# Attention and a gated FFN in one kernel: exponentials as the stationary operand, bursts of whole query groups, hardware-queue loads and turns by DMA transposes

## The chip, the cores and the metric

The kernel runs on one core of a Trainium2 chip. The metric is the time of one execution on the device in microseconds (us). All times are of one core, so no die can be compared with another: a run of such a program is called slow here only when it lies more than 1.5% above the fastest run of the same kernel.

Engines in the profile: PE is TensorE (matmul), PEld its weight loads, DVE VectorE, ACT ScalarE, POOL GpSimd, SP SyncE. SPq and the other names with q are an engine's instruction queue, which here issues DMAs. PSUM is the memory that TensorE writes to. The granted clock (PEclk) is the share of TensorE's full clock that the profile reports. QK stands for the matmuls of the scores, AV for those of exponentials and values; to turn is to transpose.

## The reference

```
k_all, v_all = concat(beacon_k, k), concat(beacon_v, v)   # 16 beacon rows ahead of 576
scores = q @ k_all.T / sqrt(64)        # 8 batches, 8 heads, 576 queries, 592 keys, depth 64
scores = where(causal, -1e9, scores)   # beacon keys are never masked
a = exp(scores - max); a /= sum(a) + 1e-9
x = (a @ v_all) as [4608 tokens, 512]
out = (relu(x @ w_gate) * (x @ w_val)) @ w_out            # 512 -> 1536 -> 512, fp32 in and out
```

## The kernel before

Two heads make a pair; there are 4 pairs a batch, 32 in all. Keys lie on the partitions of the score tile, so the exponentials p have keys on partitions and queries on columns. A pair is worked in four steps. The FFN is cut into 9 tiles of 512 tokens, each of 12 "up" pieces (8 matmuls of 512 columns) and 4 "down" pieces (12 matmuls); one piece is put between the steps of attention as filler. The exponentials are not shifted by their maximum; a check of all sums at the end leads to a general path where they are out of range.

The parts that the change and the argument touch:

```python
# values and a block of ones are stationary, the exponentials stream twice
for half in range(2):
    for a in range(2):
        w = pr.v[:kr, kt, ...] if half == 0 else ones[:kr, :]        # 64 columns
        nc.tensor.matmul(o[rows, half, ...], w, p[:kr, a, c:c + n], ...)
...
nc.vector.reciprocal(r[:, :cn], o[:, 1, :cn])                        # 128 x 256: sums, repeated 64 times
nc.vector.tensor_mul(xT[:, pr.p_idx, t0:t0 + cn], o[:, 0, :cn], r[:, :cn])
...
def part(dst, p0, p1, t, src):                  # loads cast fp32 -> bf16 on the way, issued by POOL
    nc.gpsimd.dma_start(dst[p0:p1, t, c0:c1]..., src.rearrange("h p d -> p h d"))
...
for s in range(len(work) + LAG):                # one step
    if i == 0 and pr.p_idx == 0:                # at a batch's first step: all loads of the next batch
        load_qkv(pr.b + 1, 0, H, tiles[pr.b + 1])
    qk(pr, i)
    softmax(pr, i)                              # exp on ACT, then causal masks on POOL
    ...                                         # q, k of the next pair turned on TensorE (steps 2, 3)
    if ffn: ffn.pop(0)()                        # one FFN piece
    if s >= LAG: av(*work[s - LAG])
```

## Time and profile before

| | before |
|---|---|
| time, median of 2 | 592.45 us |
| TensorE busy (per-engine table) | 447.3 of 589.1 us |
| first FFN matmul group (timeline) | 114.6 us |
| TensorE's waits on masks (table of waits) | 111.0 us in 10 waits |
| one pair of attention on TensorE (timeline) | about 3.9 us |

The page of the kernel before: the per-engine table's start, then three rows of the picture in 40 equal slices, where each digit is the busy share in tenths.

```profile
PE 447.3 (76%) x4113; PEld 227.8 (39%) x4113; DVE 259.4 (44%) x369; ACT 194.9 (33%) x273; POOL 218.1 (37%) x458
...
PE   2000037859995999599969986997799999979995
...
POOL 9998262471246125621652174217411112000000
...
DMA  4669990190059006900890099009901100100102
```

TensorE starts late (the zeros), and later dips at regular distance; POOL is at its fullest where TensorE is empty. The chain of waits, followed back from the last instruction, by engine:

```profile
PE 66%; POOL 23%; DMA 6%; DVE 2%; issue 1%; ACT 1%; ACTq 0%; POOLq 0%; DVEq 0%
```

The table of waits, TensorE's rows (total us, times, longest):

```profile
PE aux L283 <- POOL p L264: 111.0, 10, 68.8
PE aux L236 <- DMA q_sb<-in_q_dram: 9.9, 5, 8.4
```

One of the dips in the timeline (start, length, engine, line, operation, output and input, count; in brackets the idle time before it). POOL works through the loads of the next batch, and the mask of the running step comes last:

```profile
353.64 4.26 POOL L207 DMA_DIRECT2D v_sb<-in_v_dram  x5
357.80 1.02 POOL L264 TENSOR_SCALAR_AFFINE_SELECT p<-p 128x224 bf16<-128x224 bf16 x3
358.36 0.42 PE L283 MATMUL aux<-p,v_sb 128*64 128x256 bf16 x2 [7.10 <-POOL p L264]
```

So TensorE waits 7.10 us for a mask that stood behind POOL's own load issues. That the queue is first in, first out is what the Trainium skill says ("PSUM — Partial Sum Buffer", Engine vs sequencer instructions), and this trace agrees: the mask starts when the last load has been issued.

Three groups of instructions (busy us, mean ns of one, idle time before):

```profile
L290 DVE RECIPROCAL r<-aux 128x256 f32<-128x256 f32 (+1 forms) x96 | 129.8, 1352 | 160.8 <-PE aux L283 160.7
...
L283 PE MATMUL aux<-p,v_sb 128*64 128x64 bf16 (+5 forms) x832 | 72.9, 240 | 116.3 <-POOL p L264 111.0
...
L207 POOL DMA_DIRECT2D v_sb<-in_v_dram x55 | 44.3, 907 | 1.7 <-DMA k_sb<-in_k_dram 1.5
```

And one step on TensorE in the timeline: AV from 331.29 us, QK from 331.80, an FFN piece from 332.09.

```profile
331.29 0.30 PE L283 MATMUL aux<-p,v_sb 128*64 128x256 bf16 x2
...
331.80 0.36 PE L254 MATMUL s<-qT,kT 64*128 64x256 bf16 x6
332.09 2.76 PE L323 MATMUL f<-wo,hT 128*128 128x512 bf16 x12
```

### The profile page before, as it was taken

Reading aid. Unit: us, or ns where it says so; the run is one execution under the profiler, and the core shown is the slowest. Engines: PE = TensorE matmul, PEld = TensorE weight load, DVE = VectorE, ACT = ScalarE, POOL = GpSimd, SP = SyncE. Lnnn points to the kernel's source line nnn. Section 1 sums busy time; section 2 is a strip of 40 time slices with the busy share of each in tenths; the row PEclk is TensorE's granted clock in tenths of the full one; section 3 lists DMA queues with packets and bytes.
Section 4 is the critical chain, followed back from the end, with each engine's and each line's share of the span. In section 5 each row is a group of like instructions: output and inputs, shape, how many; then the busy total and the mean of one; then the engine's idle time right before and its main releaser. Section 6 shows DMA issues by size and latency. Waiting matters only on the chain.

```text
span 589.1 us, 10169 instructions
## 1 busy us (share of the span) xinstructions
PE 447.3 (76%) x4113; PEld 227.8 (39%) x4113; DVE 259.4 (44%) x369; ACT 194.9 (33%) x273; POOL 218.1 (37%) x458
## 2 busy tenths in 40 slices
PE   2000037859995999599969986997799999979995
PEld 1000025525542554355435543553355555424442
DVE  0000027536733673376437543754476576432130
ACT  2000014324432543254425442543244454322321
POOL 9998262471246125621652174217411112000000
PEclk9999999779997999799979996999699999979998
DMA  4669990190059006900890099009901100100102
GB/s 31 40 41 138 202 115 2 14 112 2 3 94 102 1 3 102 94 1 20 96 82 2 21 108 69 2 22 120 57 2 38 39 1 10 65 0 19 53 2 75
DMA packets 127029, 29.45 MB, mean 50 GB/s; under 512 B 116608, under 2 KB 122368, under 8 KB 126976
## 3 DMA queue, kind: packets, MB, share of 16 engines
q0 software_dynamic: 121408, 19.15, 44.4%
q1 hardware_dynamic: 5568, 9.59, 4.4%
q8 instruction: 34, 0.56, 0.4%
q14 instruction: 19, 0.16, 0.1%
HBM read 38.27 MB, written 9.44 MB: 81 GB/s over the span
## 4 chain that ended last, share of the span: by engine, by line
PE 66%; POOL 23%; DMA 6%; DVE 2%; issue 1%; ACT 1%; ACTq 0%; POOLq 0%; DVEq 0%
PE f L308 16%; PE f L314 15%; PE f L323 14%; PE aux L283 11%; POOL v_sb L207 8%; POOL k_sb L207 7%; PE s L254 6%; POOL q_sb L207 5%; DMA wo<-in_moe_w_out_dram 4%; PE aux L236 2%; DMA k_sb<-in_k_dram 2%; PE aux L244 2%; DVE r L290 1%; POOL p L264 1%; ACT p L261 1%
## 5 line engine op out<-in xcount | busy, mean ns | idle before, releaser
L290 DVE RECIPROCAL r<-aux 128x256 f32<-128x256 f32 (+1 forms) x96 | 129.8, 1352 | 160.8 <-PE aux L283 160.7
L261 ACT ACTIVATE p<-s 128x832 bf16<-128x832 f32 (+2 forms) x128 | 110.4, 863 | 245.3 <-PE s L254 245.3
L264 POOL TENSOR_SCALAR_AFFINE_SELECT p<-p 128x224 bf16<-128x224 bf16 (+3 forms) x224 | 67.7, 334 | 273.2 <-ACT p L261 273.2
L283 PE MATMUL aux<-p,v_sb 128*64 128x64 bf16 (+5 forms) x832 | 72.9, 240 | 116.3 <-POOL p L264 111.0
L308 PE MATMUL f<-xT,wg 128*128 128x512 bf16 x432 | 119.5, 400 | 5.0 <-DVE xT L292 4.3
L316 DVE TENSOR_TENSOR hT<-g,f 128x512 bf16<-128x512 f32 x108 | 74.0, 685 | 107.5 <-PE f L314 105.6
L314 PE MATMUL f<-xT,wv 128*128 128x512 bf16 x432 | 114.5, 389 | 0.9 <-DVE hT L316 0.9
L283 PEld LDWEIGHTS <-v_sb 128*64 128x64 bf16 (+1 forms) x832 | 45.6, 116 | 167.6 <-issue 160.1
L323 PE MATMUL f<-wo,hT 128*128 128x512 bf16 x432 | 98.4, 380 | 0.0
L311 ACT ACTIVATE g<-f 128x512 f32<-128x512 f32 x108 | 64.4, 596 | 70.1 <-PE f L308 68.7
L314 PEld LDWEIGHTS <-wv 128*128 128x128 bf16 x432 | 43.4, 100 | 64.4 <-issue 19.3
L283 PE MATMUL aux<-p,ones 128*64 128x64 bf16 (+5 forms) x832 | 64.9, 234 | 0.0
L323 PEld LDWEIGHTS <-hT 128*128 128x128 bf16 x432 | 40.1, 98 | 46.7 <-issue 1.5
L308 PEld LDWEIGHTS <-wg 128*128 128x128 bf16 x432 | 36.9, 100 | 41.6 <-issue 10.6
L254 PE MATMUL s<-qT,kT 64*128 64x64 bf16 (+3 forms) x832 | 49.2, 233 | 0.6 <-DVE kT L246 0.6
L207 POOL DMA_DIRECT2D q_sb<-in_q_dram x55 | 44.2, 890 | 8.0 <-DMA wo<-in_moe_w_out_dram 6.8
L207 POOL DMA_DIRECT2D k_sb<-in_k_dram x55 | 43.8, 858 | 5.7 <-DMA wg<-in_moe_w_gate_dram 3.5
L283 PEld LDWEIGHTS <-ones 128*64 128x64 bf16 (+1 forms) x832 | 45.2, 118 | 0.2
L326 ACT COPY ob<-f 128x512 f32<-128x512 f32 x36 | 21.1, 585 | 72.3 <-PE f L323 72.3
L207 POOL DMA_DIRECT2D v_sb<-in_v_dram x55 | 44.3, 907 | 1.7 <-DMA k_sb<-in_k_dram 1.5
L292 DVE TENSOR_TENSOR xT<-aux,r 128x256 bf16<-128x256 f32 (+1 forms) x96 | 34.3, 358 | 3.3
L254 PEld LDWEIGHTS <-kT 64*128 64x128 bf16 x832 | 25.1, 99 | 12.0 <-issue 7.1
(26 smaller groups left out, 119.4 us busy)
## 6 DMA issues: line engine op xcount, KB each, us to landing
out_dram<-ob SPq DMA_DIRECT2D x36, 256.0 KB
q_sb<-in_q_dram POOLq DMA_DIRECT2D x28, 128.0 KB, 5.7
k_sb<-in_k_dram POOLq DMA_DIRECT2D x21, 128.0 KB, 5.1
v_sb<-in_v_dram POOLq DMA_DIRECT2D x21, 128.0 KB, 4.7
wg<-in_moe_w_gate_dram POOLq DMA_DIRECT2D x4, 384.0 KB, 8.9
wv<-in_moe_w_val_dram POOLq DMA_DIRECT2D x4, 384.0 KB, 10.1
wo<-in_moe_w_out_dram POOLq DMA_DIRECT2D x1, 1536.0 KB, 20.7
rsum<-r SPq DMA_DIRECT2D x64, 2.0 KB
```

Of the source, the lines that this page charges most:

```text
L207: nc.gpsimd.dma_start(dst[p0:p1, t, c0:c1].rearrange("p (h d) -> p h d", d=D), src.rearrange("h p d -> p h d"))
L254: nc.tensor.matmul(s[:, a, c:c + n], pr.kT[rows, kt * P:(kt + 1) * P], pr.qT[rows, q0:q0 + n], start=True, stop=True)
L261: nc.scalar.activation(p[:, :, :n], pr.s[i][:, :, :n], AF.Exp, scale=scale)
L264: nc.gpsimd.affine_select(out=p[:, :, c:c + m], in_=p[:, :, c:c + m], pattern=[[0, 2], [1, m]], compare_op=ALU.is_ge, fill=0.0, base=base, ...
L283: nc.tensor.matmul(o[rows, half, q0 - cq0:q0 - cq0 + n], w, p[:kr, a, c:c + n], start=(i == first and j == 0 and half == 0), stop=(i == la ...
L290: nc.vector.reciprocal(r[:, :cn], o[:, 1, :cn])
L292: nc.vector.tensor_mul(xT[:, pr.p_idx, t0:t0 + cn], o[:, 0, :cn], r[:, :cn])
L308: nc.tensor.matmul(g, wg[:, ki, nf * P:(nf + 1) * P], xT[:, ki, m0:m0 + M_TILE], start=(ki == 0), stop=(ki == KM - 1))
L311: nc.scalar.activation(gs, g, AF.Relu)
L314: nc.tensor.matmul(u, wv[:, ki, nf * P:(nf + 1) * P], xT[:, ki, m0:m0 + M_TILE], start=(ki == 0), stop=(ki == KM - 1))
L316: nc.vector.tensor_mul(st["h"][:, nf, :], gs, u)
L323: nc.tensor.matmul(o, st["h"][:, nf, ms * P:(ms + 1) * P], wo[:, nf, :], start=(nf == 0), stop=(nf == NF - 1))
```

## The change

The intent: let the exponentials be the stationary operand, so that 65 columns of values (64 and a column of ones that gives the sum) stream past them and the sum of a query is one number; work in bursts of a whole query group instead of four steps (two bursts a pair, eight a batch; a tick is one pass of the loop, a burst and the FFN filler behind it); free POOL of load issues by loading fp32 over the hardware queue and casting on POOL or VectorE; leave the turning of x, and of q and k from batch 2 on, to DMA transposes.

The diff, cut to its core:

```diff
-                    w = pr.v[...] if half == 0 else ones[:kr, :]
-                    nc.tensor.matmul(o[rows, half, ...], w, p[:kr, a, c:c + n], ...)
+        for j, qi in enumerate(qt):                  # query blocks of the burst
+            for a in range(2):
+                for kt in kts:
+                    nc.tensor.matmul(o[:m, j, a, 0:D + 1], p[:kr, a, c:c + m],
+                                     vs[u.b % 2][:kr, kt, 2 * u.pi + a, 0:D + 1], ...)
...
+            V.reciprocal(r, o[:m, j0:j1, :, D])      # 6 or 2 numbers a partition
+            V.tensor_mul(u.x[...], o[:m, j0:j1, :, 0:D], r.unsqueeze(3).to_broadcast(...))
+        if u.last:
+            for qi in qt:                            # x is turned by DMA
+                nc.sync.dma_start_transpose(xT[...], u.x[:rn, qi, :])
...
-            nc.gpsimd.dma_start(dst[...], src...)    # cast inside the DMA
+            nc.sync.dma_start(dst[:n], rows_of(...)) # fp32 into one of 9 staging tiles; all DMAs on SP
+            G.tensor_copy(c[:n, :d_model], st[:n, :d_model])                # cast on POOL
+            nc.sync.dma_start_transpose(dst[:, :, t * P:t * P + n], c[...]) # q, k of batches 2 to 7
...
-    f_ps = ... bufs=2
+    f_ps = ... bufs=3                                # PSUM tiles of the FFN
...
+        for s in range(8): ...                       # batch 0: 8 bursts without filler
+        av(bursts[7], o_ps)                          # ends with x's five transposes
+        for c, w in wq:                              # first half of w_gate, w_val: load, cast on V
+            if c < 2: w()(V)
+        ...                                          # 5 FFN pieces, then batch 1's loads
+        GAP = 5
+        ticks = bursts[8:16] + [None] * GAP + bursts[16:] + [None]
+        for s, u in enumerate(ticks, 8):             # a tick: a burst (or none), then filler
+            budget = 1.7 if s < 16 else 4.0          # us of FFN pieces per tick: 1, then 3 up pieces
+            ...
+            for x in turned: piece_turn(x)           # DMA transposes
+            ...                                      # casts of loads asked for 1 or 2 ticks ago, new loads
```

## The prediction

> **What bounds it now.** TensorE, with three kinds of hole. The per-engine table gives it 447 us of 589 busy; the chain of waits is 66% TensorE, 23% POOL, 6% DMA.
>
> 1. Start: the timeline shows POOL issuing casting loads until 81.7 us (batch 0, all weights, batch 1) before the first mask. The wait table has TensorE waiting 68.8 us in one piece for that mask. Batch 0 without FFN filler then takes about 8.5 us a pair; FFN starts near 117 us.
> 2. At every batch start POOL issues 20-odd loads for about 13 us; the first mask stands behind them and TensorE waits about 7 us (351.3 to 358.4), six times: about 43 us.
> 3. The steady state is otherwise TensorE-bound. FFN: 9 tiles x 144 matmuls, 216 ns each (the tail's 48 in 10.37 us): 280 us. Attention, from the timeline between FFN pieces: 0.8+0.8+1.3+1.1, about 3.9 us a pair, 126 us for 32.
>
> **What changes.**
> - AV: now values and ones (64 columns) are stationary and exponentials stream twice, 1664 columns each; about 2.0 us a pair. After: 15 blocks x 2 heads = 30 matmuls of 65 moving columns, each with a 128-column weight load. The present q/k transposes have that shape and step at 50 to 70 ns: about 1.75 us. The Trainium skill ("TensorE: Matmul & The Clock Gate", LDWEIGHTS) says that load time follows columns, so short moving operands make loads the limit; this trace's loads average 100 ns but overlap.
> - TensorE transposes of q/k (about 0.8 us a pair) go to DMA for batches 2 to 7. QK drops from 26 to 16 matmuls per pair, same columns. Attention: about 2.6 us a pair, saving 1.3 x 32 = about 40 us.
> - POOL's 149 us of load issues vanish; the Trainium skill ("DMA: Bandwidth & Descriptors", Rules for kernel authors) has casting in DMA on GpSimd only, which agrees with the casting loads here, so casts become POOL/DVE copies. By the masks (128 elements 293 ns, 256 414 ns) 512 elements cost about 0.7 us; 90 pieces, about 65 us, off TensorE's path. Holes 1 and 2 nearly close.
> - DVE: the 130 us of 128x256 reciprocals become six-element ones. Hardly on the path except in batch 0.
> - Added: about 100 DMA transposes of 128 KB and fp32 loads with 256-byte pieces, all on one in-order SP queue.
>
> **Sum (estimate).** First burst near 10 us; eight bursts bound by latency at 3 to 3.5 us: 38 us; weights landed, first FFN near 44. Five FFN pieces and batch 1 (8 ticks of 3 to 3.5 us): about 85. Gap of 5 ticks: 110. Remaining FFN about 231 us plus 24 pairs x 2.6 = 62: 403. About 15 ticks have no FFN to fill (a tile lasts 6 ticks of a batch's 8); these follow ACT/POOL, about 3 us, losing 1.7 each: 26 us. End and lower clock around those holes: 15 us. Total about 446 us.
>
> **Prediction: 446 us; 80% range 420 to 488.** Faster by over 2%: 0.97; within: 0.02; slower: 0.01.
>
> **What the profile would show.** POOL load issues gone; first matmul FFN before 55 us; TensorE busy share above 85%; its waits on masks under 1.5 us apiece after batch 1; AV groups stepping 50 to 70 ns; reciprocal total under 20 us; remaining idle in ticks without FFN.
>
> **What would make it wrong.** DMA transposes slower than loads or holding up loads behind them on SP, so that q/k come late and TensorE waits on DMA; POOL casts far above 0.7 us; AV stepping at 100 ns (+40 us); early weights late (batch 0 and FFN start slip).

## The result, and the profile after

The changed kernel took 474.52 us, the median of two runs (471.21 and 477.84). The ratio to before is 0.8007, 95% interval 0.7871 to 0.8142. Ratios in this text are the mean time of one kernel's fast runs over that of the other's of the same rounds, so not quite the ratio of the medians that are quoted. A later group of six runs gave 475.80 us and the ratio 0.8019; it is the control for the experiments, and gains and losses against it are given as the difference of the two ratios times 592 us.

| | predicted | after |
|---|---|---|
| time | 446 us (420 to 488) | 474.5 us |
| first FFN matmul | near 44 us | 45.6 us |
| last burst of batch 1 | about 85 us | 108.5 us |
| FFN-only gap done | 110 us | 135.4 us |
| from there to the end | 336 us | 341 us |
| TensorE busy share | above 85% | 82% |
| step of one AV matmul | 50 to 70 ns | 30 ns |
| cast of 512 elements on POOL | 0.7 us | 0.61 us |
| reciprocals in total | under 20 us | 15.7 us |
| waits on masks after batch 1 | under 1.5 us each | up to 5.0 us |

The page of the changed kernel, the same rows:

```profile
PE 390.8 (82%) x2830; PEld 194.7 (41%) x2873; DVE 156.9 (33%) x362; ACT 188.7 (40%) x273; POOL 127.9 (27%) x288
...
PE   2760917889986855999999999689979998999975
...
POOL 4530203233134434331432333422342212000000
...
DMA  9507989646998789943893753966495004002002
```

A slice is 11.9 us. TensorE starts at once, but its fourth and sixth slices (36 to 48 and 60 to 71 us) are nearly empty, and a weak stretch follows from about 143 to 190 us. The DMA engines are nearly idle in the third slice (24 to 36 us) and full soon after. The chain:

```profile
PE 65%; DMA 14%; SPq 9%; DVE 3%; issue 3%; ACT 3%; POOL 2%; DVEq 0%; POOLq 0%; ACTq 0%
```

POOL's share fell from 23% to 2%; that of DMA rose from 6% to 14%, and SP's queue, 9%, is new. TensorE's longest waits in total:

```profile
PE f L228 <- DVE c L224: 16.8, 8, 7.6
PE o L304 <- POOL p L281: 15.5, 9, 5.0
PE f L332 <- DVE wg L257: 12.5, 2, 11.1
PE f L332 <- DMA xT<-x: 7.9, 3, 4.2
```

The groups that answer to those of before:

```profile
L304 PE MATMUL o<-vx,p 128*128 128x65 bf16 (+2 forms) x906 | 48.2, 208 | 19.0 <-POOL p L281 15.5
...
L312 DVE RECIPROCAL rall<-o 128x2 f32<-128x2 f32 (+2 forms) x90 | 15.7, 174 | 115.2 <-PE o L304 113.9
...
L493 POOL CAST c<-stg 128x512 bf16<-128x512 f32 (+2 forms) x60 | 36.1, 613 | 40.2 <-DMA stg<-in_k_dram 28.5
```

One burst on TensorE in the timeline: QK from 295.73 us, AV from 296.15, FFN from 296.53.

```profile
295.73 0.49 PE L270 MATMUL s<-qT,kT 64*128 64x368 bf16 x6
296.15 0.54 PE L304 MATMUL o<-vx,p 128*128 128x65 bf16 x12
296.53 5.34 PE L347 MATMUL f<-wo,hT 128*128 128x512 bf16 x24
```

Twelve AV matmuls, each with its own 128-column weight load, take 0.38 us to the next instruction. From the first start to the last start they are 0.54 less the 0.21 us that one lasts, over 11 steps: 30 ns.

### The profile page after: what moved, and what is told of

It is laid out like the page before. It is cut to its first block, busy times and chain, and to the rows that moved or that the text cites. A ratio compares the mean times of both kernels' runs of the same rounds, so it can differ in the third digit from the quotient of the medians.

```text
span 476.1 us, 7626 instructions
## 1 busy us (share of the span) xinstructions
PE 390.8 (82%) x2830; PEld 194.7 (41%) x2873; DVE 156.9 (33%) x362; ACT 188.7 (40%) x273; POOL 127.9 (27%) x288
## 4 chain that ended last, share of the span: by engine, by line
PE 65%; DMA 14%; SPq 9%; DVE 3%; issue 3%; ACT 3%; POOL 2%; DVEq 0%; POOLq 0%; ACTq 0%
PE f L332 18%; PE f L338 18%; PE f L347 17%; PE o L304 6%; PE s L270 5%; SPq L319 4%; DMA stg<-in_v_dram 4%; DMA stg<-in_k_dram 3%; DMA xT<-x 3%; ACT p L277 2%; DMA stg<-in_q_dram 2%; SPq L246 1%; DMA stg<-in_moe_w_out_dram 1%; DMA stg<-in_moe_w_gate_dram 1%; SPq L499 1%
## 5 line engine op out<-in xcount | busy, mean ns | idle before, releaser
L277 ACT ACTIVATE p<-s 128x992 bf16<-128x992 f32 (+2 forms) x128 | 107.4, 864 | 65.6 <-PE s L270 65.3
L281 POOL TENSOR_SCALAR_AFFINE_SELECT p<-p 128x256 bf16<-128x256 bf16 (+2 forms) x160 | 61.4, 398 | 189.9 <-ACT p L277 186.2
L304 PE MATMUL o<-vx,p 128*128 128x65 bf16 (+2 forms) x906 | 48.2, 208 | 19.0 <-POOL p L281 15.5
L304 PEld LDWEIGHTS <-p 128*128 128x128 bf16 (+2 forms) x960 | 42.3, 115 | 33.5 <-POOL p L281 18.3
L312 DVE RECIPROCAL rall<-o 128x2 f32<-128x2 f32 (+2 forms) x90 | 15.7, 174 | 115.2 <-PE o L304 113.9
L270 PE MATMUL s<-qT,kT 64*128 64x208 bf16 (+4 forms) x512 | 42.0, 280 | 6.7 <-ACT p L277 5.2
L493 POOL CAST c<-stg 128x512 bf16<-128x512 f32 (+2 forms) x60 | 36.1, 613 | 40.2 <-DMA stg<-in_k_dram 28.5
L313 DVE TENSOR_TENSOR x<-o,rall 128x128 bf16<-128x128 f32 (+2 forms) x90 | 34.6, 384 | 3.3
L250 POOL CAST vx<-stg 128x512 bf16<-128x512 f32 (+3 forms) x50 | 26.2, 529 | 13.9 <-DMA stg<-in_v_dram 13.7
L228 PE MATMUL f<-ident,c 96*128 96x96 bf16 x96 | 8.9, 252 | 23.0 <-DVE c L224 16.8
```

Source lines behind the costliest of these rows:

```text
L250: eng.tensor_copy(vs[b % 2][:n, t, h0:h1, 0:D], st[:n, :H * D].rearrange("p (h d) -> p h d", d=D)[:, h0:h1])
L270: nc.tensor.matmul(s[:, a, c:c + n], kTs[u.b % 2][rows, u.pi, kt * P:(kt + 1) * P], qTs[u.b % 2][rows, u.pi, q0:q0 + n], start=True, stop= ...
L277: A.activation(p[:, :, :cols], u.s[i][:, :, :cols], AF.Exp, scale=scale)
L281: G.affine_select(out=p[:, :, c:c + m], in_=p[:, :, c:c + m], pattern=[[0, 2], [1, m]], compare_op=ALU.is_ge, fill=0.0, base=base, channel ...
L304: nc.tensor.matmul(o[:m, j, a, 0:D + 1], p[:kr, a, c:c + m], vs[u.b % 2][:kr, kt, 2 * u.pi + a, 0:D + 1], start=first, stop=(kt == kts[-1] ...
L313: V.tensor_mul(u.x[:m, i0:i0 + j1 - j0, u.pi * P:(u.pi + 1) * P].rearrange("p j (a d) -> p j a d", a=2), o[:m, j0:j1, :, 0:D], r.unsqueeze ...
```

## The experiments

Twelve kernels ran, in three groups of four; each group had its own runs of the kernel before on the same chip. All results were correct except one. The control is the changed kernel without an edit:

> The changed kernel unedited, as the control of this group: 470 to 478 us, as its two runs so far (471.2 and 477.8).

It gave 475.80 us (469.98 to 477.56), ratio 0.8019 (0.7983 to 0.8055). Two of the six runs, 477.32 and 477.56, count as slow by the 1.5% and are not in the ratio. Its profile fell on one of them, so the traces called "the changed kernel" below are those of the first pair of runs.

### The old kernel with its loads spread

What does the change's largest single gain need? This is the kernel before, with the loads of batches 1 to 7 handed to POOL two per step, behind the masks.

```diff
-                    load_qkv(pr.b + 1, 0, H, tiles[pr.b + 1])       # ahead of the step
+            if i == 0 and pr.p_idx == 0 and pr.b + 1 < B:           # behind qk, softmax and av
+                load_qkv(pr.b + 1, 0, H, tiles[pr.b + 1], later)    # only listed
+            for _ in range(2):
+                if later: later.pop(0)()                            # two issues a step
```

> The kernel before, with one thing changed: the 17 to 22 casting loads of the next batch are handed to POOL two per step, behind the step's masks, instead of all at the batch's start. Theory (masks stood behind load issues on POOL: six holes of 7 us, and about 25 us of the start, where batch 1's loads come before the first mask): 592 falls to 515 to 540 us. Rival (the holes only move, because q and k then come late or every step's mask is delayed): gain under 25 us.

Measured: 522.79 us, ratio 0.8834 (0.8810 to 0.8857). The table of waits of this run:

```profile
PE aux L288 <- POOL p L269: 55.2, 5, 41.4
```

Ten waits on masks have become five, and the longest is 41.4 instead of 68.8 us. The stretch from 200 to 400 us (columns: window, length, busy us of PE, PEld, DVE, ACT and POOL with counts, granted clock, DMA share, GB/s), first before, then here:

```profile
200.00:400.00 200.00, 178.48 (x1751) 91.20 (x1750) 110.63 (x157) 81.06 (x113) 72.16 (x166) 0.94 0.49 47
```

```profile
200.00:400.00 200.00, 197.58 (x2031) 101.70 (x2032) 126.26 (x182) 94.17 (x132) 89.41 (x199) 1.00 0.63 60
```

POOL does no less in this stretch than before (89.4 against 72.2 us), and TensorE still gains 19 us: not the amount of POOL's work mattered, but what stood ahead of the masks in its order. The granted clock rose as well, from 0.94 to 1.00. After the hole of 7.10 us shown above, four FFN matmuls of the old kernel step 1.68 us (360.39 to 362.07 us) where they step 0.86 us a little later (364.83 to 365.69), so a hole cost more than its length; how much of the gain this makes is not separated. The theory held. Some 69 us, against 118 for the whole change, could be had by spreading these loads alone.

### The old kernel without reciprocals

```diff
-            nc.vector.reciprocal(r[:, :cn], o[:, 1, :cn])
+            nc.vector.tensor_copy(r[:, :cn], o[:, 1, :cn])    # wrong numbers on purpose
```

> The kernel before, with the reciprocal of the broadcast sums replaced by a copy (wrong numbers on purpose): takes about 100 us of VectorE time away. The prediction said that this time is hardly on the path except in batch 0: then 582 to 590 us. Rival (VectorE holds the two shared PSUM buffers of outputs and transposes, so it is on the path in every pair): 570 us or less.

Measured: 581.55 us, ratio 0.9822 (0.9797 to 0.9847). Its output is wrong, which doesn't matter for the time. VectorE's busy time fell from 259.4 to 167.2 us, and 92 us less work there gave 10.5 us, at the edge of the expected 582 us. The prediction's reading held in the main: most of it was off the path.

### AV issued twice

The changed kernel, with every AV group issued two times over. This measures what AV costs by adding it once more.

```diff
-        first = True
-        for j, qi in enumerate(qt):
+        for again in range(2):
+         first = True
+         for j, qi in enumerate(qt):
```

> The changed kernel, with every group of AV matmuls issued twice (same result): the cost of AV measured by itself. The timeline shows groups of 12 such matmuls with 0.33 to 0.38 us from one group's start to the next instruction's start, about 30 ns each; if TensorE is the limit nearly everywhere, 960 more cost 25 to 35 us: 500 to 510 us. At the 50 to 70 ns that the prediction took it would be 48 to 67 us: 522 to 541. If attention mostly hides in waits, under 15 us.

Measured: 494.51 us, ratio 0.8352 (0.8331 to 0.8373), which is 19.7 us above the control (which ran in another group, on another chip), less than expected. The timeline gives the step again:

```profile
305.71 0.90 PE L305 MATMUL o<-vx,p 128*128 128x65 bf16 x24
306.45 5.34 PE L348 MATMUL f<-wo,hT 128*128 128x512 bf16 x24
```

24 matmuls take 0.74 us where 12 took 0.38, so 30 ns each; 960 more are 29 us of TensorE, of which 20 us reached the time (waits on masks fell from 15.5 to 11.3 us). The prediction had taken 50 to 70 ns, from the q/k transposes of the old kernel, and thought weight loads set that pace. Here they don't. The Trainium skill ("TensorE: Matmul & The Clock Gate", Back-to-back issue gap) gives, for a single matmul at the full clock, a gap of N/2.4 + 2.5 ns for N moving columns: an estimate of 29.6 ns for 65. The measured 30 ns is that, although every matmul has its own weight load, recorded at 105 ns each. The transposes had 128 moving columns. The columns set the pace here, not the loads, as the run below that turns q and k on TensorE again shows. There eight transposes of 128 moving columns take 0.61 us (at 227.94 us) and four take 0.39 us (at 234.46), so 55 ns each. They too have a 128-column load each, and with the same loads 65 columns take 30 ns.

### Weight loads earlier

In the changed kernel SP issues all DMAs in order. At the end of batch 0 its queue looked like this:

```profile
33.41 7.32 SPq L319 DMA_TRANSPOSE xT<-x  x5
40.83 0.53 SPq L256 DMA_DIRECT2D stg<-in_moe_w_gate_dram  x1
```

The weights for the first FFN piece are asked for only after five transposes of x, which wait for batch 0's last burst.

```diff
+            if s == 4:                                   # inside batch 0
+                wcasts = [w() for c, w in wq if c < 2]   # loads only
...
-                w()(V)                                   # after av(bursts[7]): load and cast
+        for cast in wcasts: cast(V)
```

> The changed kernel, with the first eight weight loads issued inside batch 0 (after the last q/k pair of that batch is asked for) instead of after its last burst. Theory A (order on the one SP queue: these loads stand behind five DMA transposes of x that wait for batch 0's last burst, while the DMA engines are about 20% busy from 20 to 40 us): the weights are asked for by about 25 us instead of 41, batch 1's loads follow about 12 to 18 us earlier, the TensorE hole from 60 to 82 us mostly closes; time 452 to 462 us instead of 474.5. The first FFN matmul moves little (about 43 us), since x itself has to be turned first. Theory B (the DMA rate, or the nine staging tiles, bound the start whatever the order): batch 1 still comes at the same time, gain under 4 us.

Measured: 468.42 us, ratio 0.7887 (0.7849 to 0.7925), between the two theories; against the control, which ran in another group on another chip, it is 7.8 us. The weights were now cast at 36 to 40 us, and the first FFN matmul came at 42.4 instead of 45.6 us. But batch 1's loads still left at 41.3 us, behind the same transposes, and later weight loads waited for staging tiles whose VectorE casts stood behind FFN work in VectorE's order. The next run treats these too.

### The start reordered

```diff
+            if s == 4: wcasts = [w() for c, w in wq if c < 2]
+            if s >= 6:                                   # weights cast between batch 0's last bursts
+                for _ in range(4): wcasts.pop(0)(V)
+            if s == 6:                                   # batch 1's first loads, ahead of x's transposes
+                bk = beacons_k(1)
+                kq1 = [(pair_kq(1, p, k), pair_kq(1, p, q)) for p in range(2)]
         av(bursts[7], o_ps)
+        turn_beacons(bk, 1)                              # ahead of the first FFN piece
+        for p in range(2): pair_turn(1, p, *kq1[p])
```

> The changed kernel, its start reordered: the first eight weight loads and batch 1's beacons and first two q/k pairs are asked for before batch 0's x is turned, the weights are cast between the last bursts of batch 0, and batch 1's first two pairs are turned before the first FFN matmul. The first run of this kind (weight loads alone) gained about 6 us, because batch 1's loads still stood behind the five transposes on SP and because staging tiles were then freed only by VectorE casts that stand behind five FFN pieces. If these two orders are the whole cause of the late start, the fifth FFN piece is done near 52 us, batch 1 runs 15 to 25 us earlier than in the changed kernel, and the time is 450 to 460 us. If the DMA rate is the limit, 465 us or more.

Measured: 463.63 us, ratio 0.7805 (0.7766 to 0.7844), 12.7 us below the control and between the two theories. The first two 40 us of the changed kernel and of this one:

```profile
0.00:40.00 40.00, 19.46 (x236) 13.89 (x236) 15.39 (x40) 14.13 (x17) 16.32 (x44) 0.87 0.55 103
40.00:80.00 40.00, 18.87 (x87) 7.85 (x90) 18.50 (x32) 5.07 (x8) 5.86 (x12) 0.63 0.95 235
```

```profile
0.00:40.00 40.00, 20.83 (x240) 15.02 (x240) 20.46 (x51) 14.21 (x17) 17.64 (x45) 1.00 0.88 203
40.00:80.00 40.00, 26.16 (x177) 12.94 (x178) 18.89 (x34) 9.82 (x15) 9.91 (x21) 0.87 0.72 198
```

The DMA engines move 203 instead of 103 GB/s in the first stretch, and TensorE has 26.2 instead of 18.9 us of work in the second. In the timeline the last QK of batch 1 starts at 93.1 instead of 105.1 us: the gain is from here. The order on SP and in the staging tiles caused at least about half of the 23 us by which batch 1 came later than predicted. For the other half there is this: from 40 to 80 us the changed kernel's DMA engines are 95% busy at 235 GB/s, and even here the last QK of batch 1 starts only at 93.1 us. That the DMA rate sets the rest is argued from these numbers, not shown, and the reordered run's trace has a rival. From 40 to 60 us its DMA engines are 60% busy at 168 GB/s. Its longest wait of TensorE, 9.5 us to 66.80, ends with the cast of k for batch 1's third pair, whose load is issued only at 60.97 us, behind four weight loads (56.3 to 58.1) and after a cast of weights at 60.38. So order and staging tiles may hold back part of this half too.

### Thinner filler

```diff
-            budget = 1.7 if s < 16 else 4.0
+            budget = 1.7 if s < 16 else (4.0 if u is None else 3.0)
```

Three up pieces a tick finish a tile in six ticks; a batch has eight. Two a tick last all eight.

> The changed kernel, with the FFN filler of a tick cut from three pieces to two wherever a burst runs beside it (from batch 2 on); one number changed. The prediction put 26 us down to ticks without filler, which follow the latency of exponential, mask and AV. If that is right, a tile now fills all eight ticks of a batch, the slow ticks of batches 3 to 7 vanish, and 8 to 18 us are saved: 456 to 467 us. If idle ticks cost little, or the work merely moves to the end, within 4 us of the control.

Measured: 456.27 us, ratio 0.7720 (0.7696 to 0.7744), 17.7 us below the control from one number. From 200 to 400 us, first the changed kernel, then this one:

```profile
200.00:400.00 200.00, 187.93 (x1429) 92.17 (x1450) 64.48 (x154) 97.52 (x143) 60.40 (x135) 0.97 0.59 118
```

```profile
200.00:400.00 200.00, 200.00 (x1566) 97.99 (x1565) 71.60 (x172) 105.65 (x154) 60.30 (x135) 1.00 0.60 118
```

TensorE is now busy through all 200 us. So the lack of filler did cost much of what was predicted, but mostly not by the path predicted, the latency of exponential, mask and AV. TensorE's two longest rows of waits in these 200 us of the changed kernel:

```profile
PE f L332 <- DMA xT<-x: 6.8, 2, 4.2
PE s L270 <- ACT p L277: 3.0, 6, 0.7
```

Only 3.0 us are waits on exponentials. The 6.8 us are two waits (until 311.38 and 357.99 us) where the filler has run out and the next FFN tile waits for the DMA turn of x. After each, groups of four FFN matmuls step 1.7 us for a while instead of 0.86 (313.04 to 314.74 us). In the thinner run this stretch has no wait at all. What is left of idle time lies before 200 us, where this edit changed nothing (TensorE busy 60.6 of the 80 us from 120 to 200, and 61.3 in the changed kernel).

### Turning q and k on TensorE again

```diff
-            nc.sync.dma_start_transpose(dst[:, :, t * P:t * P + n], c[:n, :d_model])
+            tp = f_ps.tile([P, NP, P], BF16, name="f")
+            for j in range(NP):
+                nc.tensor.transpose(tp[:, j, :n], c[:n, j * P:(j + 1) * P], ident[:n, :n])
+            V.tensor_copy(dst[:, :, t * P:t * P + n], tp[:, :, :n])
```

> The changed kernel, with the 60 DMA transposes of q and k of batches 2 to 7 undone: the same loads and casts, but 232 to 240 TensorE transposes into PSUM and 60 VectorE copies instead. If the DMA turn earns what the prediction said (about 0.8 us of TensorE a pair, 24 pairs: 19 us, less in the short blocks), this is 10 to 20 us slower than the control. If the transposes on the SP queue (1.2 us of issue each) and on the DMA engines (busy 0.9 or more from 120 to 200 us) hold up the loads of batches 2 and 3, what is lost on TensorE is won back there and it is within 5 us of the control, or faster.

Measured: 466.01 us, ratio 0.7880 (0.7846 to 0.7914): 8.2 us faster than the control. Undoing one part of the change gained. TensorE had 240 matmuls more and VectorE 60 copies (22 us), yet the stretch where batches 2 and 3 are loaded ran better. TensorE's waits from 120 to 200 us, in the changed kernel and here:

```profile
PE o L304 <- POOL p L281: 14.2, 7, 5.0
```

```profile
PE o L304 <- POOL p L281: 2.3, 2, 1.8
```

TensorE was busy 73.5 instead of 61.3 of those 80 us, at a granted clock of 0.94 instead of 0.79. The 60 transposes cost two things. On SP, one takes about 1.2 us of issue in the timeline (the five of x above fill 7.3 us with the gaps between them), some 72 us in all, where a load of 256 KB takes 0.57 us. On the DMA engines, the queue's share fell from 60.0% of 476.1 us to 52.4% of 464.3, or from 286 to 243 us: 42 us on the mean engine for 7.2 MB. Whether the issue or the engines' time hurt is open, since this run removes both; and how much of the gain is the higher clock is not separated.

### Casts a tick later

Do slow loads reach TensorE because masks stand behind waiting casts on POOL? This leaves the DMA transposes and gives the casts of batch 3 and later one tick more.

```diff
-                        inflight.append((s + (1 if early else 2), piece_load(...)))
+                        inflight.append((s + (1 if early else 3), piece_load(...)))
```

> The changed kernel, with POOL's casts of batch 3 and later asked for three ticks after the load instead of two. Turning q and k on TensorE instead of by DMA (the run before this) saved about 8 us and cut TensorE's waits on masks from 15.5 to 3.6 us. Theory: slow loads reach TensorE through POOL, where the masks of a burst stand behind casts that wait for a load; a tick more of slack then removes most of these waits without touching the DMA transposes: 464 to 471 us. Rival (the waits come from the loads of batch 2, which this leaves as they are, or only move to the DMA turns, which come a tick later): within 3 us of the control's 475.8.

Measured: 476.69 us, ratio 0.8052 (0.8023 to 0.8080), not distinguishable from the control's 0.8019 (0.7983 to 0.8055). The theory fell, and the table of waits from 120 to 200 us tells how:

```profile
PE f L332 <- DMA xT<-x: 6.0, 1, 6.0
PE s L270 <- DMA qT<-c: 4.8, 1, 4.8
PE o L304 <- POOL p L281: 4.2, 3, 3.5
```

The waits on masks went from 14.2 to 4.2 us as hoped, and 10.8 us of new waits took their place, for x and for q that had not been turned in time. So POOL's order was not the whole cause. The new waits end with DMAs, but the edit also makes the DMA turns of q and k a tick later and so may have made some of them itself: that slow DMAs stand behind both is argued, not shown.

### Two PSUM tiles for the FFN

```diff
-    f_ps = ... bufs=3
+    f_ps = ... bufs=2
```

> The changed kernel with two instead of three PSUM tiles for the FFN, as the kernel before had; one number changed, a part of the change that its few words do not name. In the tail of the kernel before, a pair of gate and value groups steps 1.87 us; in the changed kernel 1.73 us. If that is the tile count, 108 pairs cost about 15 us more: 484 to 494 us. If not, within 4 us of the control's 475.8.

Measured: 480.19 us, ratio 0.8116 (0.8101 to 0.8131), 5.7 us above the control. The step of a pair of gate and value groups in the FFN-only tail (changed kernel, then this run):

```profile
440.20 1.03 PE L332 MATMUL f<-xT,wg 128*128 128x512 bf16 x4
441.07 1.03 PE L338 MATMUL f<-xT,wv 128*128 128x512 bf16 x4
441.93 1.03 PE L332 MATMUL f<-xT,wg 128*128 128x512 bf16 x4
```

```profile
440.16 1.03 PE L332 MATMUL f<-xT,wg 128*128 128x512 bf16 x4
441.18 1.02 PE L338 MATMUL f<-xT,wv 128*128 128x512 bf16 x4
442.04 1.03 PE L332 MATMUL f<-xT,wg 128*128 128x512 bf16 x4
```

1.73 against 1.88 us, as expected, so the mechanism is right; but 108 pairs do not all pay it. Less than half of the 15 us arrived. Where bursts stand between the pieces the third tile seems to matter less; no run separates that.

### The edits together

> Three edits that each gained, together: the start reordered, the filler thinner, q and k turned on TensorE. Alone they gained about 12, 18 and 8 us over the control. If they act on different stretches (start, batches 3 to 7, batch 2), the sum holds: 475.8 less 38, 434 to 442 us. If they remove the same idle time, 445 to 455 us.

Measured: 442.17 us, ratio 0.7476 (0.7457 to 0.7494). That is 32.1 us below the control, of the 38.6 that the three gained alone, just short of the expected sum: they act on mostly different stretches.

The last edit also cuts the pause ahead of batch 2:

```diff
-        GAP = 5
+        GAP = 3
-            if s >= 14:      # loads of batch 2 begin
+            if s >= 12:
```

> The same three edits, and the pause of FFN-only ticks ahead of batch 2 cut from five to three, its loads begun two ticks earlier. If the pause uses up filler that batch 2 then lacks, 3 to 8 us faster than the three edits alone. If the loads of batch 2 can't come earlier because batch 1's and the weights fill the DMA engines, equal or slower.

Measured: 434.67 us (434.31 to 436.60), ratio 0.7364 (0.7348 to 0.7380), and the fastest of all: 6.6 us below the three edits, as expected, 26% below the kernel before and 8% below the changed one. Its per-engine line:

```profile
PE 385.1 (89%) x3113; PEld 201.5 (47%) x3113; DVE 176.5 (41%) x422; ACT 189.6 (44%) x273; POOL 129.4 (30%) x288
```

## Why the prediction was right or wrong

The time, 474.5 us, lies inside the range of 420 to 488 and 28 us above the central 446.

- **Holes on POOL: right.** The two holes were read from the waits and priced at 43 us and a large part of the start. Spreading the loads alone gave 69 us.
- **Batch 0 and first FFN: right in the number, in part by luck.** "First FFN near 44" was 45.6. Batch 0's last AV group starts at 33.5 us, earlier than the 38 of the sum, and then TensorE waits 11.1 us for the weights, where the sum left 6.
- **"Five FFN pieces and batch 1 (8 ticks of 3 to 3.5 us): about 85": this step failed.** It was 108.5 us, 23 of the 28 us missing; 22 of them fell in this step, which took 62.9 instead of 41 us. The tick length was counted from engine work, as if the inputs of batch 1 and the weights were there. They were asked for late, behind x's transposes on SP, and held back by staging tiles; 12.7 us came back when that order was mended, and the cause of the rest stays open. The prediction had named "early weights late" and loads held up on SP among what would make it wrong, but put nothing for them into the sum.
- **Gap: right.** 26.9 us from 108.5 to 135.4, against 25.
- **AV: the term was mis-sized.** Thirty matmuls were put at 1.75 us a pair; at 30 ns they are 0.9. The old AV took about 2.0 us, so this swap saves TensorE about 1.1 us a pair (an estimate from the two timelines), not 0.25. The inference that weight loads limit short matmuls was wrong.
- **Moving q and k turns to DMA as a saving: wrong in sign.** The sum counted 0.8 us of TensorE a pair as saved and nothing for SP's queue and the DMA engines. The turns did leave TensorE, but undoing this made the kernel 8.2 us faster.
- **Waits on masks "under 1.5 us apiece": wrong.** Up to 5.0 us; POOL now waits for loads ahead of the masks, and where that order is eased, DMA waits replace it.
- **Ticks without filler: right that they cost, 26 us predicted and 17.7 removed by one number; the path was mostly another.** Of 12.1 us idle from 200 to 400 us, 6.8 are waits for the DMA turn of x and 3.0 on exponentials; the lower clock after the waits comes on top.
- **Reciprocals hardly on the path: right**, 10.5 us of some 92.

From 135 us to the end the sum came out nearly right (341 against 336) by luck, because two errors offset each other. Attention took about 1.9 instead of 2.6 us a pair (an estimate from the timeline: 0.42 + 0.38 for one burst, 0.50 + 0.64 for the other), some 16 us less over 24 pairs. Idle time and a lower clock took more than the 41 us of the sum: TensorE is idle for 38.7 us of this part, 22 of them in waits for masks and for x, and the granted clock is 0.74 from 135 to 200 us. The third PSUM tile, 5.7 us, was in the diff and not itemised.

How the 47 us between the spread old kernel (523) and the changed one (476) divide among AV, start and the rest is not separated by these runs.

## What to carry to other kernels

Before counting on an engine's speed, look at what stands ahead of the critical instruction in each in-order queue: masks behind load issues on POOL cost 69 us here, weights and batch 1's loads behind transposes on SP and behind staging tiles about 13. Spread filler so that it lasts until the next filler is ready; moving it from three pieces a tick to two was worth 18 us. Price a move to DMA with its issue time and its effect on the loads that share the queue, and when a wait is removed, look at which wait takes its place before calling it the cause.

## What the Trainium skill lacked or had wrong

- "TensorE: Matmul & The Clock Gate", Back-to-back issue gap: it says that in a stream of weight-load and matmul pairs N=128 sustains about 81 ns a matmul, and that the N/2.4 + 2.5 formula under-counts there. Here pairs with 65 moving columns stepped 30 ns, as the formula has it (an estimate of 29.6), and, in the run that turns q and k on TensorE again, pairs with 128 columns 55 ns, with a load of 128 columns for each.
- "Advanced Engine Details and Errata", X-Bar Transpose (TRN2): transposing DMAs are said to be as fast as regular ones. (The same page's table under DGE: Hardware vs Software calls the hardware path's transposes less efficient, without a figure.) In this kernel SP spent about 1.2 us issuing one of 128 KB against 0.57 us for a load of 256 KB, and removing 60 of them took 42 us from the mean DMA engine for 7.2 MB (5.9 us a MB), while all that remained took 243 us for 52.5 MB (4.6 us a MB). What remained has 40 transposes of x and loads in pieces of 256 bytes in it, so no run here compares transposes with large plain DMAs.
- "DMA: Bandwidth & Descriptors", Rules for kernel authors: its table says which engine is to issue a DMA that casts. It mentions the time of the issuing sequencer without a figure, and no rule there warns that the engine's own compute waits behind the issues. Here the casting loads of q, k and v took POOL about 0.9 us each, and a mask behind them held TensorE up for 7.10 us at one batch.
